# One more half of a depthwise convolution moved from TensorE to VectorE, one more sequence gated by sigmoid, and all instruction orders written anew

## The chip, the core and the metric

The kernel runs on one core of a Trainium2 chip. The core has five engines, each with its own in-order instruction queue: TensorE (PE) for matrix products and transposes, VectorE (DVE) and ScalarE (ACT) for elementwise work, GpSimd (POOL) for a few copies and for issuing loads, and SyncE (SP) for issuing DMAs. [...] The time is the device time of one execution in microseconds (us). Before the change it is 213.52 us, the median of three runs (213.04 to 213.94).

## The reference

Eight sequences (b = 0 to 7) of 576 rows go through attention with pooled keys and values, and then through a gated feed-forward block with a short convolution:

```python
k_p = k.reshape(B, H, Sp, 8, D).mean(axis=3)          # 576 keys -> 72
v_p = v.reshape(B, H, Sp, 8, D).mean(axis=3)
attn = softmax(scale * q @ k_p^T)                     # per head, 576 x 72
x = (attn @ v_p), the heads put side by side          # 576 x 512
h = np.maximum(x @ w_in, 0.0)                         # 576 x 1024
conv_out[s] = sum over k of conv_w[k] * h[s + k - 1]  # three taps, channel by channel
out = (h * 1 / (1 + exp(-conv_out))) @ w_out          # 576 x 512
```

Inputs and output are float32; the kernel computes in bfloat16 with float32 sums.

## The kernel before

**Tiles.** The sequences go in four pairs g = 0 to 3. Attention works on tiles (g, t) of 128 rows, nine or ten to a pair. One tile takes: scores on PE (line 607 when the array is used in quarters, line 620 when whole), the maximum on DVE (L633), the subtraction on DVE (L645) or, for pair 0, on PE (L653), exp on ACT (L682), a transpose by PE (L692) or by a DMA from SP (L701), the product with the pooled values on PE (L717), a reciprocal on DVE (L730), and the division on DVE (L745) or, as eight small instructions, on ACT (L738). The result x is transposed into xT.

**The feed-forward block.** The 1024 channels of a sequence are eight blocks fb of 128, in two halves f4 of four blocks. For each block PE computes the projection (`ffn_in`, L775, two times four matrix products), and ACT evicts it through a ReLU into hT (`ffn_relu`, L784). Then comes the convolution, in one of two ways:

- On PE (`ffn_conv`, L939): 32 small products by diagonal matrices for two blocks. ACT evicts them through tanh or sigmoid (L964), half of them into gT and half into a buffer tg, from which DVE brings them into gT (`ffn_gate`, L979 and L981).
- On DVE (`ffn_tap`, L911), for the halves listed in `Graph.TAPS`: two instructions for each block, h times a ratio of weights added to the running sum, which is held in float32 in tg. The rows of a sequence are interleaved, so the ends of hT must first get a copy of 63 columns from the other end (`ffn_wrap`, L859 and L860, one pair for two blocks, on POOL or ACT). ACT reads tg and writes the gate into gT (`ffn_tap_tanh`, L921).

The gate is a sigmoid. It is computed as tanh of half the argument, with the factor 0.5 put into the ReLU and a "+1" on DVE (L926 for tap halves, part of L979 and L981 otherwise), or, for the halves in `Graph.SIG`, as a sigmoid with no "+1". Exp and tanh are used under one activation table and sigmoid under another, so a sigmoid must stand behind every exp of the program; the last lines of the kernel add that dependence. `ffn_times` (L989) multiplies the gate by h, four blocks at once. When both halves of a sequence are gated, PE computes its output tiles (`ffn_out`, L997, eight products of 512 columns), DVE or ACT copies them out of PSUM (L1008), and SP or ACT issues the stores.

**Buffers and order.** Small rings of buffers are shared: three of tg, two of hT, two of gT. The program is a graph of operations. `Graph.ORDER` lists them in the order in which they are emitted, with the engine for each (a number is twice the operation's index plus the choice of engine, -1 is a filler product on PE, L424). `Graph.FORMS` sets the use of the PE array in whole or in parts, and `Graph.PLACES` the buffer of each operation. So the three tables fix each engine's queue. `pm`, `ident` and other constants are made in the first microseconds, while the first q and k arrive.

Of the kernel before, what the change touches and what calls it, by code (L numbers as in the profile page):

```python
# [33 lines left out]
class Graph:  # L34
# [25 lines left out]
    TAPS = ((4, 1), (5, 0), (5, 1), (6, 0), (6, 1), (7, 0), (7, 1))  # L60
# [8 lines left out]
    SIG = ((6, 0), (6, 1), (7, 0), (7, 1))  # L69
# [57 lines left out]
    )  # L127
    FORMS = (
        0, 0, 0, 0, 1, 1, 1, 1, 0, 0, 0, 0, 0, 1, 1, 0, 1, 1, 0, 0, 1, 0, 1, 0, 0, 0, 0, 1, 0, 0, 0, 1, 1, 1, 1, 1, 1, 1, 0, 1,
    )  # L130
    PLACES = (
# [51 lines left out]
def kernel(  # L183
# [1125 lines left out]
    def add_ffn(b, w):  # L1309
# [28 lines left out]
        for f4 in range(n_fb // 4 if b in Graph.WRAP else 0):  # L1338
            if (b, f4) not in Graph.TAPS and b not in Graph.SIXTEEN:
                continue  # L1340
# [7 lines left out]
        for f4 in range(n_fb // 4):  # L1348
            if (b, f4) not in Graph.TAPS:
                continue  # L1350
# [148 lines left out]
```

## Time and profile before

| | |
|---|---|
| median of 3 runs | 213.52 us (213.04 to 213.94) |
| the profiled execution | 213.68 us, its span 211.7 us |
| busy in the span | PE 198.9, DVE 190.5, ACT 167.2, POOL 36.7 us |
| granted TensorE clock, mean | 0.995 |
| HBM | 32.52 MB read, 9.44 MB written |

The span goes from the first instruction to the last. Busy time of an engine is the union of its instructions' durations; "xN" counts them, and a mean in ns is that of one instruction. In a row of a group, the part behind the second bar is the idle time of the engine just before these instructions and what ended it. A row of the windows view gives, for one stretch of time, its length and each engine's busy time in it, then the clock, the share of DMA time and the rate. A row of the chain or of the timeline gives start, length and what ran, with repeated instructions merged. "PEld" is the loading of weights, which overlaps PE's products.

### The profile page before, as it was taken

The numbers are of one execution on the slowest core, as the hardware profiler recorded it, in microseconds if no ns is written. First come the engines' busy times: TensorE is split into PE (matmuls) and PEld (weight loads), VectorE is DVE, ScalarE is ACT, GpSimd is POOL, SyncE is SP. The second block draws the span as 40 slices with busy tenths as digits, with TensorE's granted clock in tenths as the row PEclk, the third lists the DMA queues.
The fourth block names the chain that finished last, engine by engine and source line by source line (L and its number), as shares of the span: only waits on it lengthen the run. The fifth ranks groups of instructions, "written<-read, shape, count | busy, mean of one in ns | idle before, by whom it ended". The sixth has DMA issues, their size and how long they took to land.

```text
span 211.7 us, 6644 instructions
## 1 busy us (share of the span) xinstructions
PE 198.9 (94%) x2726; PEld 136.4 (64%) x2746; DVE 190.5 (90%) x338; ACT 167.2 (79%) x345; POOL 36.7 (17%) x60
## 2 busy tenths in 40 slices
PE   4899999999999999999999899999999999999990
PEld 1468788765688876776778675666666656654450
DVE  7879988999999999999998989999999999999520
ACT  2558677998999869999979977989899997889030
POOL 8604630052131110200000021000014400202000
PEclk9999999999999999999999999999999999999997
DMA  6999999999999999879663646756646626204985
GB/s 212 222 205 206 208 206 208 208 207 205 208 206 208 202 179 202 177 139 156 130 92 69 147 96 78 173 104 151 122 96 133 113 64 149 53 0 103 261 259 171
DMA packets 48834, 33.47 MB, mean 158 GB/s; under 512 B 28300, under 2 KB 43812, under 8 KB 48804
## 3 DMA queue, kind: packets, MB, share of 16 engines
q0 software_dynamic: 15216, 15.40, 44.6%
q1 hardware_dynamic: 32432, 15.93, 35.9%
q10 hardware_dynamic: 1156, 1.72, 2.8%
q8 instruction: 21, 0.34, 0.6%
q14 instruction: 9, 0.07, 0.1%
HBM read 32.52 MB, written 9.44 MB: 198 GB/s over the span
## 4 chain that ended last, share of the span: by engine, by line
PE 68%; DVE 19%; issue 5%; ACT 4%; DMA 2%; DVEq 0%; ACTq 0%
PE psum L997 25%; PE psum L775 22%; PE psum L717 5%; PE psum L939 3%; DVE negm L633 3%; DVE v L511 2%; PE psum L692 2%; DMA eT<-e 2%; PE psum L424 2%; DVE sd L645 2%; DVE gT L981 2%; PE psum L620 2%; DVE gT L989 1%; PE psum L653 1%; PE psum L762 1%
## 5 line engine op out<-in xcount | busy, mean ns | idle before, releaser
L775 PE MATMUL psum<-xT,w_in_sb 128*128 128x288 bf16 x512 | 72.0, 286 | 0.2
L997 PE MATMUL psum<-w_out_sb,gT 128*128 128x512 bf16 (+1 forms) x276 | 65.6, 373 | 1.4 <-issue 0.6
L775 PEld LDWEIGHTS <-w_in_sb 128*128 128x128 bf16 x512 | 47.8, 98 | 15.3
L784 ACT ACTIVATE hT<-psum 128x576 bf16<-128x576 f32 x64 | 41.1, 669 | 8.0 <-PE psum L775 7.8
L997 PEld LDWEIGHTS <-gT 128*128 128x128 bf16 x296 | 27.5, 98 | 26.5 <-DVE gT L989 0.5
L633 DVE TENSOR_REDUCE negm<-psum 128x8 f32<-128x576 f32 (+2 forms) x37 | 27.4, 750 | 2.0 <-ACT e L682 0.9
L921 ACT ACTIVATE gT<-tg,ratio 128x576 bf16<-128x576 f32 x28 | 21.6, 795 | 2.2 <-DVE tg L911 2.1
L911 DVE SCALAR_TENSOR_TENSOR tg<-hT,ratio,tg 128x576 f32<-128x576 bf16 x28 | 22.3, 813 | 0.7
L911 DVE SCALAR_TENSOR_TENSOR tg<-hT,ratio 128x576 f32<-128x576 bf16 x28 | 22.2, 812 | 0.2 <-ACT gT L921 0.2
L859 POOL COPY hT<-hT 128x126 bf16<-128x126 bf16 x7 | 5.7, 808 | 93.8 <-ACT hT L784 74.9
L989 DVE TENSOR_TENSOR gT<-gT,hT 128x2304 bf16<-128x2304 bf16 x16 | 21.6, 1354 | 0.2
L645 DVE TENSOR_TENSOR sd<-psum,negm 128x576 f32<-128x576 f32 x27 | 19.9, 751 | 0.6
L717 PE MATMUL psum<-vm,eT 128*128 128x65 bf16 (+5 forms) x240 | 19.0, 222 | 0.9 <-DMA eT<-e 0.9
L738 ACT ACTIVATE x<-psum,r 128x64 bf16<-128x64 f32 (+1 forms) x80 | 17.6, 352 | 2.8 <-DVE r L730 2.7
L682 ACT ACTIVATE e<-sd 128x576 bf16<-128x576 f32 x27 | 18.6, 703 | 0.4 <-DVE sd L645 0.2
L745 DVE TENSOR_TENSOR x<-psum,r 128x512 bf16<-128x512 f32 (+1 forms) x27 | 18.2, 682 | 0.5
L717 PEld LDWEIGHTS <-eT 128*128 128x128 bf16 (+1 forms) x240 | 15.1, 100 | 5.3 <-DMA eT<-e 1.7
L939 PE MATMUL psum<-hT,dw 64*64 64x288 bf16 (+2 forms) x576 | 17.0, 256 | 0.3 <-ACT qT L559 0.2
L939 PEld LDWEIGHTS <-dw 64*64 64x64 bf16 x576 | 13.9, 107 | 3.4 <-issue 2.3
L424 PE MATMUL psum<-gT 128*128 128x448 bf16 x40 | 13.1, 433 | 3.2 <-DVE gT L1106 2.8
L1008 ACT COPY osb<-psum 128x512 f32<-128x512 f32 x24 | 14.3, 600 | 1.2 <-PE psum L997 1.2
L511 DVE TENSOR_TENSOR v<-v 128x1280 bf16<-128x1280 bf16 (+2 forms) x24 | 12.9, 538 | 0.2
(95 smaller groups left out, 244.8 us busy)
## 6 DMA issues: line engine op xcount, KB each, us to landing
out_dram<-osb SPq DMA_DIRECT2D x54, 128.0 KB, 2.5
v<-in_v_dram POOLq DMA_DIRECT2D x8, 512.0 KB, 12.6
qp<-in_q_dram POOLq DMA_DIRECT2D x7, 576.0 KB, 15.3
kk<-in_k_dram POOLq DMA_DIRECT2D x3, 1152.0 KB, 13.7
out_dram<-qp ACTq DMA_DIRECT2D x12, 128.0 KB, 3.4
hT<-in_k_dram SPq DMA_DIRECT2D x2, 576.0 KB, 5.2
w_in_sb<-in_moe_w_in_dram POOLq DMA_DIRECT2D x2, 512.0 KB, 13.7
w_out_sb<-in_moe_w_out_dram POOLq DMA_DIRECT2D x1, 1024.0 KB, 23.7
```

The source lines that it names most:

```text
L633: nc.vector.tensor_reduce(out=a["m"][0:rows], in_=a["s"][0:rows, :, 0:2 * KW].rearrange("p a (h s) -> p a h s", s=Sp), axis=AX.X, op=OP.ma ...
L645: nc.vector.tensor_tensor(out=a["d"][0:rows], in0=a["s"][0:rows, :, 0:2 * KW].rearrange("p a (h s) -> p a h s", s=Sp), in1=a["m"][0:rows]. ...
L682: nc.scalar.activation(out=dst, in_=src, func=ACT.Exp,)
L717: nc.tensor.matmul(out=a["o"][lo:hi, h // 4, (h % 4) * (D + 1):(h % 4 + x1 - x0) * (D + 1)], lhsT=a["eT"][:, j, lo:hi], rhs=buf("vm", b)[: ...
L745: nc.vector.tensor_tensor(out=a["x"][0:rows].rearrange("p (a h d) -> p a h d", a=2, d=D), in0=ov[:, :, :, 0:D], in1=r[0:rows].unsqueeze(3) ...
L775: nc.tensor.matmul(out=banks(ps)[:, j, 0:SC], lhsT=w_in_block(dc, fb), rhs=buf("xT", g)[:, dc, i * S + j * SC:i * S + (j + 1) * SC], start ...
L784: nc.scalar.activation(out=h_of(b)[:, fb].rearrange("p (a s) -> p a s", a=2), in_=banks(ps)[:, :, 0:SC], func=ACT.Relu, scale=1.0 if (b, f ...
L911: nc.vector.scalar_tensor_tensor(out=acc, in0=h, scalar=w, in1=acc if tap else mid, op0=OP.mult, op1=OP.add)
L921: nc.scalar.activation(out=gate, in_=acc_of(b, fb, ps), func=squash(b, fb), scale=ratio[:, 1, fb:fb + 1])
L939: nc.tensor.matmul(out=banks(pss[r ^ c])[c * D:(c + 1) * D, j, lo:hi], lhsT=dw[r * D:(r + 1) * D, tap * n_fb + fb, :], rhs=hT[r * D:(r + 1 ...
L989: nc.vector.tensor_tensor(out=gate, in0=gate, in1=h_of(b)[:, four], op=OP.mult)
L997: nc.tensor.matmul(out=bank(ps)[0:rows, columns], lhsT=buf("gT", g)[:, fb, t * P:t * P + rows], rhs=w_out_sb[:, fb, columns], start=(fb == 0),
```

## The change

`Graph.TAPS` gets the half (4, 0): the first four blocks of sequence 4 are now convolved on DVE too, so that all eight halves of sequences 4 to 7 are. `Graph.SIG` gets both halves of sequence 5: their gates are sigmoids, so they stand behind every exp and need no "+1". `ORDER`, `FORMS` and `PLACES` are new from end to end. The tables are one line longer, so every line number behind them moves by one (L911 is L912 in the changed kernel).

```diff
-    TAPS = ((4, 1), (5, 0), (5, 1), (6, 0), (6, 1), (7, 0), (7, 1))
+    TAPS = ((4, 0), (4, 1), (5, 0), (5, 1), (6, 0), (6, 1), (7, 0), (7, 1))
...
-    SIG = ((6, 0), (6, 1), (7, 0), (7, 1))
+    SIG = ((5, 0), (5, 1), (6, 0), (6, 1), (7, 0), (7, 1))
...
     ORDER = (
-        0, 12, 10, 24, 16, 4, 44, 28, 8, 36, 14, 32, 46, 19, -1, -1, -1, -1, 21, 7,
...
+        0, 12, 10, 24, 16, 4, 44, 28, 8, 36, 14, 32, 46, 42, 40, -1, 66, -1, -1, -1,
...
```

Counted over the program, PE loses 64 convolution products, DVE gets 8 taps and loses one L926, one L979 and two L981; of the 16 pairs of wraps (14 before) POOL has 14 (7 before) and ACT 2 (7 before). PE has 40 fillers in both. The tables also deal out the copies and divisions that either DVE or ACT can do, as the prediction lists.

Two places in the queues. The first is ACT's queue where it changes from exp and tanh to sigmoid. gT_121 belongs to sequences 4 and 5 here, gT_122 to 6 and 7; e is the result of an exp, hT that of a ReLU, osb an output tile. Before:

```order
L738 ACTIVATE x_107<-psum,r_113 128x64 x8
L784 ACTIVATE hT_117<-psum 128x576
L1008 COPY osb_123<-psum 128x512
L921 ACT_TABLE_LOAD
L921 ACTIVATE gT_122<-tg_118,ratio 128x576
L784 ACTIVATE hT_117<-psum 128x576 x2
L859 COPY hT_117<-hT_117 128x2x63
L860 COPY hT_117<-hT_117 128x2x63
L1008 COPY osb_124<-psum 128x512
L921 ACTIVATE gT_122<-tg_119,ratio 128x576
```

After:

```order
L785 ACTIVATE hT_117<-psum 128x576 x3
L683 ACTIVATE e_98<-sd_130 128x2x2x144
L1009 COPY osb_126<-psum 128x512
L683 ACTIVATE e_101<-sd_129 128x2x2x144
L922 ACT_TABLE_LOAD
L922 ACTIVATE gT_121<-tg_118,ratio 128x576
L1009 COPY osb_125<-psum 128x512
L922 ACTIVATE gT_121<-tg_120,ratio 128x576
```

Before, the load of the table stands in the gates of pair 3 (gT_122), fifteen operations behind the last exp, and the copies at the ends of hT are among ACT's work. After, it stands directly behind the last exp, and the first sigmoids write gT_121: they are those of sequence 5.

The second place is DVE's queue where sequence 4 is gated. Before:

```order
L911 SCALAR_TENSOR_TENSOR tg_118<-hT_116,ratio 128x576
L730 RECIPROCAL r_111<-psum 128x8
L911 SCALAR_TENSOR_TENSOR tg_118<-hT_116,ratio,tg_118 128x576
L911 SCALAR_TENSOR_TENSOR tg_119<-hT_116,ratio,tg_119 128x576
L979 TENSOR_SCALAR gT_121<-gT_121 128x2x576
L981 TENSOR_SCALAR gT_121<-tg_120 64x2x576 x2
L989 TENSOR_TENSOR gT_121<-gT_121,hT_117 128x4x576
L633 TENSOR_REDUCE negm_96<-psum 128x8
```

After:

```order
L912 SCALAR_TENSOR_TENSOR tg_118<-hT_117,ratio 128x576
L912 SCALAR_TENSOR_TENSOR tg_120<-hT_116,ratio,tg_120 128x576
L646 TENSOR_TENSOR sd_130<-psum,negm_96 128x576
L912 SCALAR_TENSOR_TENSOR tg_119<-hT_117,ratio 128x576
L990 TENSOR_TENSOR gT_121<-gT_121,hT_116 128x4x576
L927 TENSOR_SCALAR gT_121<-gT_121 128x4x576
L912 SCALAR_TENSOR_TENSOR tg_120<-hT_117,ratio 128x576
L912 SCALAR_TENSOR_TENSOR tg_118<-hT_117,ratio,tg_118 128x576
L990 TENSOR_TENSOR gT_121<-gT_121,hT_116 128x4x576
L912 SCALAR_TENSOR_TENSOR tg_120<-hT_117,ratio,tg_120 128x576
```

Before, one half of sequence 4 arrives from PE's convolution and is brought into gT by an L979 and two L981, between taps of sequence 5 (hT_116) and ahead of maxima of attention. After (where hT_116 is sequence 4's and hT_117 sequence 5's), both halves have come by taps, a full-width "+1" (L927) and a product (L990) follow for each, and no attention stands between the two products.

More of the change, by code (lines that the diff above doesn't have):

```diff
@@ L72 @@
     ORDER = (
[54 rows of a table removed]
[55 rows of a table added]
     )
     FORMS = (
-        0, 0, 0, 0, 1, 1, 1, 1, 0, 0, 0, 0, 0, 1, 1, 0, 1, 1, 0, 0, 1, 0, 1, 0, 0, 0, 0, 1, 0, 0, 0, 1, 1, 1, 1, 1, 1, 1, 0, 1,
+        1, 1, 0, 0, 0, 0, 1, 0, 0, 0, 0, 1, 1, 1, 0, 0, 1, 0, 0, 0, 1, 1, 1, 0, 0, 0, 0, 1, 1, 0, 0, 1, 1, 1, 1, 1, 1, 1, 1, 0,
     )
     PLACES = (
[18 rows of a table removed]
[18 rows of a table added]
     )
```

143 rows, old and new, of tables (ORDER, PLACES) are left out of this document.

## The prediction

> **What bounds the kernel now.** I read the page's busy times first, then the chain, then the engines' busy time by stretch.
>
> ```profile
> span 211.7 us, 6644 instructions
> ...
> PE 198.9 (94%) x2726; PEld 136.4 (64%) x2746; DVE 190.5 (90%) x338; ACT 167.2 (79%) x345; POOL 36.7 (17%) x60
> ```
>
> ```profile
> PE 68%; DVE 19%; issue 5%; ACT 4%; DMA 2%; DVEq 0%; ACTq 0%
> ```
>
> Two engines are almost full, TensorE (PE, 94%) and VectorE (DVE, 90%), and ScalarE (ACT) isn't far behind. The chain is mostly PE's. A share of the span hides the stages, so here are the stretches that the chain's changes of engine suggest (time, its length, busy time of PE, its weight loads, DVE, ACT and POOL):
>
> ```profile
> 0.00:28.10 28.10, 24.41 (x434) 16.61 (x434) 23.68 (x64) 16.50 (x28) 14.56 (x27) 1.00 1.09 210
> 28.10:72.40 44.30, 43.58 (x734) 33.24 (x730) 42.33 (x82) 38.95 (x73) 9.02 (x17) 1.00 1.23 207
> 72.40:111.00 38.60, 37.72 (x677) 27.95 (x681) 37.74 (x65) 34.22 (x77) 2.47 (x3) 1.00 0.94 155
> ...
> 157.00:174.50 17.50, 17.39 (x119) 10.90 (x119) 17.29 (x26) 17.44 (x41) 4.75 (x6) 1.00 0.51 100
> ...
> 197.00:206.00 9.00, 8.82 (x48) 4.62 (x48) 3.08 (x6) 2.24 (x4) 0.00 (x0) 1.00 0.89 270
> 206.00:211.70 5.70, 0.00 (x0) 0.00 (x0) 0.34 (x1) 0.00 (x0) 0.00 (x0) 0.81 0.58 174
> ```
>
> The start (to 28.1) has room on every engine. From 28.1 to 72.4 PE is busy for 43.58 of 44.30; from 72.4 to 111.0 PE and DVE both miss less than a microsecond. After the last gate, at 197, PE works 8.8 us more on five tiles of output, and 5.7 us of copy and store end the span. Those two belong to the end whatever happens before it. The stretch that the change rebuilds runs from the first projection of sequence 4 (115.4) to the last gate (197):
>
> ```profile
> 0.00:115.40 115.40, 110.12 (x1948) 81.50 (x1957) 107.51 (x217) 93.72 (x183) 26.05 (x46) 1.00 1.06 184
> ...
> 115.40:197.00 81.60, 79.95 (x741) 50.27 (x742) 79.61 (x117) 71.29 (x159) 10.62 (x14) 1.00 0.54 108
> ```
>
> It lasts 81.60 us; PE works 79.95 of them and DVE 79.61. Neither leaves 2 us idle, ACT 10.3. So a microsecond taken from PE alone is worth nothing there unless DVE gets through as fast, and one put on DVE costs about one.
>
> **The change, part by part.** (1) TensorE loses the two convolution calls of sequence 4's first half. One call in the chain:
>
> ```profile
> 69.36 0.87 PE psum L939 x32
> ```
>
> The longest calls there take 0.94, this one 0.87; two are 1.7 us less on PE. In the rebuilt stretch PE then has 79.95 - 1.7 = 78.2 us of work. What hides the gain is DVE, next.
>
> (2) DVE gains eight tap instructions (line 911, two for each of four blocks), ACT gets four L921 activations out of SBUF in place of four out of PSUM, which is a few tenths. The half of sequence 4 loses its two-part gate (one L979, two L981) and takes a full L926; both L926 of sequence 5 go, since a sigmoid needs no "+1".
>
> ```profile
> L911 DVE SCALAR_TENSOR_TENSOR tg<-hT,ratio,tg 128x576 f32<-128x576 bf16 x28 | 22.3, 813 | 0.7
> L911 DVE SCALAR_TENSOR_TENSOR tg<-hT,ratio 128x576 f32<-128x576 bf16 x28 | 22.2, 812 | 0.2 <-ACT gT L921 0.2
> L921 ACT ACTIVATE gT<-tg,ratio 128x576 bf16<-128x576 f32 x28 | 21.6, 795 | 2.2 <-DVE tg L911 2.1
> ...
> L981 DVE TENSOR_SCALAR gT<-tg 64x1152 bf16<-64x1152 bf16 x18 | 8.9, 494 | 0.2
> ...
> L979 DVE TENSOR_SCALAR gT<-gT 128x1152 bf16<-128x1152 bf16 x9 | 4.0, 445 | 0.0
> ...
> L926 DVE TENSOR_SCALAR gT<-gT 128x2304 bf16<-128x2304 bf16 x3 | 2.3, 755 | 0.0
> ```
>
> The 56 taps overlap a little; by the windows view of that line they fill
>
> ```profile
> 0.00:211.70 211.70, 43.58 (x56) 0.99 0.84 158
> ```
>
> 43.58 / 56 = 0.78 us each. Eight: +6.2. Gates: -(0.45 + 2 x 0.49) - 0.76 = -2.2 (three L926 become two). Net +4.0 on DVE if nothing else moved.
>
> (3) The new order also deals out work between DVE and ACT anew. Inside the rebuilt stretch DVE drops three divisions (L745) and one output copy (L1008) to ACT, one maximum (L633) is done earlier, and one mask product (L515) falls into it:
>
> ```profile
> L633 DVE TENSOR_REDUCE negm<-psum 128x8 f32<-128x576 f32 x27 | 20.0, 750 | 0.7 <-ACT e L682 0.5
> ...
> L745 DVE TENSOR_TENSOR x<-psum,r 128x512 bf16<-128x512 f32 x26 | 17.6, 682 | 0.5
> L738 ACT ACTIVATE x<-psum,r 128x64 bf16<-128x64 f32 x72 | 15.9, 357 | 2.4 <-DVE r L730 2.3
> ...
> L515 DVE TENSOR_TENSOR vm<-v,mask_wide 128x960 bf16<-128x960 bf16 x8 | 5.2, 653 | 0.1
> ...
> L1008 DVE COPY osb<-psum 128x512 f32<-128x512 f32 x3 | 2.0, 682 | 1.2 <-DMA out_dram<-osb 1.2
> ```
>
> -3 x 0.68 - 0.68 - 0.75 + 0.65 = -2.8. Instructions overlap by some hundredths, so with (2) DVE has +1.2 to +1.5 in the stretch; I take +1.4. ACT gets three divisions of eight L738 each, which at 15.9 / 72 = 0.22 are +5.3, and loses five pairs of wraps, 0.6 each (part 5): about +2.4 on 71.3 of 81.6, still under PE and DVE over the whole stretch.
>
> So DVE has 79.61 + 1.4 = 81.0 us of work there and PE 78.2: DVE is the bound by itself. Its idle time decides the rest. At the old idle time, 81.60 - 79.61 = 2.0, the stretch takes 83.0 (+1.4); with none 81.0 (-0.6). Some of the old 2.0 came from waits for PE, which now has 2.8 us to spare, so I take 1.3 of idle and 82.3: +0.7. That is nearer to the upper end because an in-order queue of taps, ACT results and gates never ran without waits in any row above.
>
> (4) Before 115.4 the new order leaves the same attention and projections on PE, three score tiles in the quarter form instead of the full one and a key preparation in halves: a few tenths. DVE there takes two divisions and a maximum more (2 x 0.68 + 0.75), gives up two L770, one L706, one L515 and a pair of L559 (0.74 and a short one of about half its width, so about 0.4), and takes casts that ACT had: two L456 of full width, one L504, two L306 of qp, for one L306 of kk.
>
> ```profile
> L559 DVE COPY qT<-psum 128x1152 bf16<-128x1152 bf16 x4 | 3.0, 740 | 0.0
> L770 DVE COPY xT<-psum 128x512 bf16<-128x512 bf16 x7 | 2.9, 420 | 0.4 <-PE psum L762 0.2
> ...
> L706 DVE COPY eT<-psum 128x640 bf16<-128x640 bf16 x3 | 1.4, 483 | 0.0
> ...
> L504 ACT CAST kT<-psum 128x576 bf16<-128x576 f32 x2 | 1.3, 636 | 0.0
> ...
> L306 ACT CAST qp<-hT 128x512 bf16<-128x512 f32 x2 | 1.1, 615 | 3.7 <-DMA hT<-in_q_dram 3.7
> ...
> L306 DVE CAST kk<-hT 128x1152 bf16<-128x1152 f32 x1 | 1.0, 985 | 0.0
> ...
> L456 DVE CAST kT<-psum 64x144 bf16<-64x144 f32 x1 | 0.3, 299 | 0.9 <-PE psum L431 0.9
> ```
>
> The known ones are 2.1 - 0.84 - 0.48 - 0.65 - 1.15 = -1.0. Three forms have no row on DVE: L456 between 0.30 (half the width) and 0.6, L504 between ACT's 0.64 and 0.99, a qp cast between half of 0.99 and ACT's 0.62. That is 2 x 0.45 + 0.8 + 2 x 0.55 - 0.99 = +1.8 with the middles, +0.25 to +0.45 on either side. DVE: +0.8. It has 115.40 - 107.51 = 7.9 us idle there, most of it in the start, where those casts lie. Fully hidden it is 0, and the earlier first projection could give 0.5; not hidden it is +0.8. I take +0.2. POOL's loads come in another order (q of sequence 6 is last now), but all are issued before the rebuilt stretch. SP issues two more of the stores at the end and ACT two fewer; the DMA share of 0.54 in that stretch leaves room for either.
>
> (5) Wraps (lines 859 and 860). Before, 7 pairs ran on ACT and 7 on POOL; now 14 of 16 run on POOL, a queue with no other work by then.
>
> ```profile
> L859 ACT COPY hT<-hT 128x126 bf16<-128x126 bf16 x7 | 2.2, 310 | 0.1
> ```
>
> ```profile
> 156.34 0.29 POOL L860 COPY hT<-hT 128x126 bf16<-128x126 bf16 x1
> ...
> 190.02 0.88 POOL L859 COPY hT<-hT 128x126 bf16<-128x126 bf16 x1 [8.88 <-issue]
> ```
>
> A POOL copy takes 0.29 when it is alone and 0.88 beside taps, so a pair takes up to 1.8 us against 0.6 on ACT, and the tap behind it waits that much longer after its ReLU. In the order only two places have little between ReLU, wrap and tap (sequence 6's blocks 0 and 1, sequence 7's blocks 4 and 5): within the idle time of (3).
>
> Does POOL slow DVE? Two taps without a POOL copy beside them, two with, and the last gates:
>
> ```profile
> 188.35 1.54 DVE L911 SCALAR_TENSOR_TENSOR tg<-hT,ratio 128x576 f32<-128x576 bf16 x2
> 189.93 1.58 DVE L911 SCALAR_TENSOR_TENSOR tg<-hT,ratio,tg 128x576 f32<-128x576 bf16 x2
> ...
> 194.38 2.61 DVE L989 TENSOR_TENSOR gT<-gT,hT 128x2304 bf16<-128x2304 bf16 x2
> ```
>
> 1.54 against 1.58: 0.04 for two copies, so 14 more wrap copies cost DVE at most 0.3, in (3)'s idle time. [...]
>
> Sum: (3) +0.7, (4) +0.2, tail 0: +0.9 us on an execution of 213.68 (span 211.7 and 2.0 around it), 0.16 above the median of the runs. Against the median, 213.52 + 0.9 = **214.4 us**.
>
> **Rivals.** *DVE keeps pace (faster).* PE's lead lets DVE run nearly without waits: idle under 0.3 in the stretch (-0.3 to -0.6) and a start that is up to 0.5 to 1 us shorter, because the first projection stands a few operations earlier in the order. That gives 212.0 to 213.2. For it: PE gets 2.8 us of slack, and DVE managed 39.5 of 40.0 in the last stretch before 197. Against it: it needs DVE to be nearly perfect for 80 us. It decides when DVE's idle time there falls under 0.5.
>
> [...]
>
> *The sigmoid switch (slower).* All exps must precede the first sigmoid. Before, the switch came in sequence 6's gates, fifteen ACT operations after the last exp; now it stands right behind it, with
>
> ```profile
> L921 ACT ACT_TABLE_LOAD x1 | 1.3, 1283 | 0.0
> ```
>
> and sequence 5's gates behind that. The taps have three buffers, so DVE stops when three blocks wait for their activation. If the last two attention tiles come 1 to 3 us late, everything behind them does: 215 to 217. ACT was already busy for 17.44 of 17.50 from 157.0 to 174.5, where this lands.
>
> **How the numbers follow.** DVE-bound as summed, 213.4 to 215.6: 0.50. DVE keeps pace: 0.24. Wraps or ports: 0.13. Sigmoid switch: 0.08. Something in the start (load order, clock): 0.05. Half a per cent of the median, 1.07 us, is about what a measurement can tell, so faster means under 212.45 and slower over 214.59. The first case gives 0.28 the same and 0.22 slower; the second 0.20 faster and 0.04 same; the next two are slower (0.21); the last 0.02 faster, 0.03 slower. Faster 0.22, same 0.32, slower 0.46. The range 212.1 to 217.0 leaves a tenth outside at each end.
>
> **What would show it.** Right: L939 x512 and two calls fewer; 64 taps at 0.81; from sequence 4's first projection to the last gate 82 to 83 us with DVE over 98% busy and PE 2 to 4 us idle, its idle time released by DVE gT L990; a chain that runs through DVE to the last gate, then 8.8 + 5.7 us as before. Wrong: PE as full as before (the rival that keeps pace), DVE idle over 3 us with POOL hT or ACT gT as releaser (wraps, switch), or a first projection a microsecond away from 28.

## The result: 0.5% slower, with the loss and the gain in other places than predicted

The changed kernel takes 214.62 us (median of 20 runs, 213.20 to 216.68) beside 213.34 for the kernel before (20 runs, 212.73 to 214.66). The ratio is 1.0054 with an interval of 1.0028 to 1.0081. The profiled execution took 213.85 us, near the fast end of its runs, 0.17 more than the profiled one before. From its page, the span, the busy times and the chain by engine:

```profile
span 212.2 us, 6550 instructions
...
PE 198.1 (93%) x2668; PEld 135.1 (64%) x2688; DVE 191.5 (90%) x339; ACT 169.7 (80%) x345; POOL 44.1 (21%) x74
...
PE 59%; ACT 15%; DVE 11%; DMA 7%; issue 5%; SPq 1%; DVEq 0%; ACTq 0%
```

PE and DVE are about as full as before. The chain has more of ACT and of DMA in it and less of PE and of DVE (11% where it was 19%). The windows view by the prediction's stretches (time, length, busy time of PE, weight loads, DVE, ACT, POOL, then clock, DMA share and GB/s) shows where the time went:

```profile
0.00:117.99 117.99, 110.24 (x1966) 81.32 (x1975) 108.51 (x218) 93.41 (x168) 26.19 (x46) 1.00 1.06 183
117.99:198.00 80.01, 79.05 (x660) 49.19 (x666) 79.54 (x117) 74.49 (x174) 17.91 (x28) 1.00 0.53 112
198.00:207.00 9.00, 8.83 (x48) 4.62 (x48) 3.08 (x6) 1.76 (x3) 0.00 (x0) 1.00 0.87 229
207.00:212.20 5.20, 0.00 (x0) 0.00 (x0) 0.35 (x1) 0.00 (x0) 0.00 (x0) 0.97 0.52 152
```

| stretch of the profiled execution | before | after | predicted | measured |
|---|---|---|---|---|
| start to sequence 4's first projection | 115.40 | 117.99 | +0.2 | +2.6 |
| from there to the last gate (rebuilt) | 81.60 | 80.01 | +0.7 | -1.6 |
| tail | 14.7 | 14.2 | 0 | -0.5 |

These are one execution of each kernel, and two things have to be known to read them. In both, 20 of PE's products in `ffn_out` have no record (276 of 296), ten of them in the rebuilt stretch, so PE's busy time there reads about 0.6 us too low in both (the kernel with five entries changed, below, has them all and shows 79.64). And about half of the 1.6 us gained in the rebuilt stretch is a wait of the profiled execution before: PE waits 0.9 us there for a transposed eT by DMA, at 121 us. Two further kernels below, which are the kernel before with an edit, don't have that wait, and their stretch takes 80.73 and 80.75 us.

So in these two profiles the rebuilt stretch gained 1.6 us and the part ahead of it lost 2.6. In that first part PE has the same work as before (110.24 against 110.12) and 7.75 us of idle time in place of 5.28: 2.5 more. The waits of PE from sequence 0's first projection (27.75) on, after:

```profile
PE psum L608 <- issue: 1.5, 1, 1.5
PE psum L542 <- issue: 1.0, 1, 1.0
PE psum L763 <- ACT kT L484: 0.2, 1, 0.2
```

and before, over the same part of the work:

```profile
PE psum L997 <- issue: 0.5, 3, 0.2
PE psum L424 <- ACT kT L483: 0.3, 1, 0.3
```

Two single waits, 1.0 and 1.5 us, add up to the 2.5. "issue" means that nothing in the profile ended them. In the timeline of the longer one PE stops in the middle of one tile's scores, six products done and ten to go, and DVE then waits for PE:

```profile
91.20 0.25 PE L608 MATMUL psum<-kT,qT 64*64 64x72 bf16 x6
92.93 0.17 PEld L608 LDWEIGHTS <-qT 64*64 64x64 bf16 x10 [1.59 <-issue]
92.93 0.28 PE L608 MATMUL psum<-kT,qT 64*64 64x72 bf16 x10 [1.48 <-issue]
...
93.32 0.76 DVE L634 TENSOR_REDUCE negm<-psum 128x8 f32<-128x576 f32 x1 [1.41 <-PE psum L608]
```

**A cause that could be tried.** PE's own instructions may be what it waits for. The page lists a DMA queue of kind "instruction" (q8) with 21 packets of 0.34 MB in all, which is 16 KB each. PE's queue has 5377 instructions, which is 21 times 256 and one more, so one packet may be one page of 256. In the trace's DMA records one such packet is under way just ahead of each of the two stops; these are the rows of the DMA view from 43.90 to 44.95 and from 90.35 to 91.60:

```profile
q8 instruction: 1, 0.02, 5.8%
```

(the same row in both). The packets end at 44.90 and at 91.56, and PE goes on at 46.27 and at 92.93, which is 1.37 us later both times. The instructions that PE waits for are number 1471 and about number 3006 of its queue, six pages apart (1535 = 6 x 256 less one). That each packet brings PE one page is the author's reading of these counts and times, and the runs below test it.

At the pages that PE entered up to 121 us in this trace, the packet with the next page starts after the entry: at most 0.8 us after it from 99 to 121 us, and 1.2 to 3.8 us after it before that, where the loads and transposes keep the DMA engines full (a share of 1.29 from 86.56 to 90.39). The packet takes about 1 us (0.9 to 1.4 here), and 1.4 more pass at the two stops until PE goes on. So, as an estimate from these three times (3.8 + 1 + 1.4), a page has to last PE some 6 us while the DMA engines are full. The page that PE entered at 86.56 held one preparation of q in the quarter form and half of another, one score tile in that form and the first part of the next (a preparation has 72 instructions and a score tile 32, where the whole form has 36 and 8), a convolution call and projections. PE was through with it in 4.9 us. The kernel before has more instructions on PE, but the ends of its pages lie elsewhere. The closest page there was ready at 45.2 by the same count (its packet ended at 43.82, and 1.4 more), 0.3 us before PE came to it.

### The profile page after: what moved, and what is told of

Same layout as the page of the kernel before. It is cut to its first block, busy times and chain, and to the rows that moved or that the text cites. A ratio compares the mean times of both kernels' runs of the same rounds, so it can differ in the third digit from the quotient of the medians.

```text
span 212.2 us, 6550 instructions
## 1 busy us (share of the span) xinstructions
PE 198.1 (93%) x2668; PEld 135.1 (64%) x2688; DVE 191.5 (90%) x339; ACT 169.7 (80%) x345; POOL 44.1 (21%) x74
## 3 DMA queue, kind: packets, MB, share of 16 engines
q10 hardware_dynamic: 996, 1.45, 2.5%
## 4 chain that ended last, share of the span: by engine, by line
PE 59%; ACT 15%; DVE 11%; DMA 7%; issue 5%; SPq 1%; DVEq 0%; ACTq 0%
PE psum L998 19%; PE psum L776 19%; PE psum L940 4%; PE psum L718 4%; DMA hT<-in_k_dram 3%; DVE tg L912 3%; ACT gT L922 2%; PE psum L425 2%; DVE x L746 2%; PE psum L608 2%; ACT x L739 2%; PE psum L621 2%; ACT hT L785 2%; DMA eT<-e 2%; DMA out_dram<-osb 2%
## 5 line engine op out<-in xcount | busy, mean ns | idle before, releaser
L785 ACT ACTIVATE hT<-psum 128x576 bf16<-128x576 f32 x64 | 42.4, 690 | 6.9 <-PE psum L776 6.3
L860 POOL COPY hT<-hT 128x126 bf16<-128x126 bf16 x14 | 10.1, 719 | 91.0 <-ACT hT L785 79.9
L922 ACT ACTIVATE gT<-tg,ratio 128x576 bf16<-128x576 f32 x32 | 25.6, 825 | 2.2 <-DVE tg L912 2.2
L912 DVE SCALAR_TENSOR_TENSOR tg<-hT,ratio 128x576 f32<-128x576 bf16 x32 | 25.3, 815 | 0.1
L912 DVE SCALAR_TENSOR_TENSOR tg<-hT,ratio,tg 128x576 f32<-128x576 bf16 x32 | 25.1, 818 | 0.0
L990 DVE TENSOR_TENSOR gT<-gT,hT 128x2304 bf16<-128x2304 bf16 x16 | 21.5, 1348 | 0.3 <-ACT gT L922 0.2
L683 ACT ACTIVATE e<-sd 128x576 bf16<-128x576 f32 x27 | 19.7, 745 | 1.2 <-DVE sd L646 1.2
L739 ACT ACTIVATE x<-psum,r 128x64 bf16<-128x64 f32 (+1 forms) x88 | 19.6, 415 | 0.2 <-DVE r L731 0.2
L1009 ACT COPY osb<-psum 128x512 f32<-128x512 f32 x26 | 16.1, 623 | 4.5 <-PE psum L998 2.0
L940 PE MATMUL psum<-hT,dw 64*64 64x288 bf16 (+2 forms) x512 | 15.1, 256 | 0.2 <-ACT qT L560 0.2
L940 PEld LDWEIGHTS <-dw 64*64 64x64 bf16 x512 | 12.4, 107 | 2.0 <-issue 1.5
## 6 DMA issues: line engine op xcount, KB each, us to landing
kk<-in_k_dram POOLq DMA_DIRECT2D x3, 1152.0 KB, 14.7
```

What stands on the lines that cost most here:

```text
L739: nc.scalar.activation(out=a["x"][0:rows, n * D:(n + 1) * D], in_=ov[:, n // 4, n % 4, 0:D], func=ACT.Identity, scale=r[0:rows, n // 4, n ...
L785: nc.scalar.activation(out=h_of(b)[:, fb].rearrange("p (a s) -> p a s", a=2), in_=banks(ps)[:, :, 0:SC], func=ACT.Relu, scale=1.0 if (b, f ...
L912: nc.vector.scalar_tensor_tensor(out=acc, in0=h, scalar=w, in1=acc if tap else mid, op0=OP.mult, op1=OP.add)
L922: nc.scalar.activation(out=gate, in_=acc_of(b, fb, ps), func=squash(b, fb), scale=ratio[:, 1, fb:fb + 1])
L940: nc.tensor.matmul(out=banks(pss[r ^ c])[c * D:(c + 1) * D, j, lo:hi], lhsT=dw[r * D:(r + 1) * D, tap * n_fb + fb, :], rhs=hT[r * D:(r + 1 ...
L990: nc.vector.tensor_tensor(out=gate, in0=gate, in1=h_of(b)[:, four], op=OP.mult)
```

## The experiments

Two theories for the 2.6 us. **Instructions come late**: the two stops are ends of pages, and whatever moves the page ends or thins the work there moves the time. **The order itself**: DVE's extra work ahead of 118 and the new order of loads and stores cost the time, and page ends don't matter. Each ratio below is to the kernel before, run beside that kernel; the times themselves come from several sets of runs, so compare the ratios.

### Whole forms everywhere, in both kernels

The row of the changed kernel; the row of the kernel before gets the same zeros.

```diff
     FORMS = (
-        1, 1, 0, 0, 0, 0, 1, 0, 0, 0, 0, 1, 1, 1, 0, 0, 1, 0, 0, 0, 1, 1, 1, 0, 0, 0, 0, 1, 1, 0, 0, 1, 1, 1, 1, 1, 1, 1, 1, 0,
+        0, 0, 0, 0, 0, 0, 0, 0, 0, 0, 0, 0, 0, 0, 0, 0, 0, 0, 0, 0, 0, 0, 0, 0, 0, 0, 0, 0, 0, 0, 0, 0, 0, 0, 0, 0, 0, 0, 0, 0,
```

> The changed kernel with every entry of FORMS at 0: scores and preparations use the array whole or in halves, so TensorE has 4833 instructions in its queue instead of 5377; nothing else differs. Theory 'instructions come late': the changed kernel's trace has two places (45.27 to 46.27 and 91.45 to 92.93) where PE stops inside one operation for nothing that the profile shows, and both end 1.37 us after a 16 KB packet of the instruction queue; with fewer instructions to the microsecond both go away: 2.0 to 2.6 us less than the changed kernel in a profile, first projection of sequence 4 at 115.5 instead of 117.99, no stop of PE over 0.4 us without a releaser between 28 and 118. Rival 'the order itself' (DVE's extra work before 118 and the new order of loads and stores): the form of the products matters little, -0.3 to +0.5 us.

> The kernel before with every entry of FORMS at 0 (4961 instructions on PE instead of 5493). Theory 'instructions come late': by the page times of its trace no page of the kernel before came late (the closest arrived 0.3 us before it was needed, at 45), so there is nothing to gain: -0.3 to +0.5 us. A theory that the quarter forms are slow in themselves expects a gain here of the same size as in the changed kernel.

Measured: the changed kernel 215.26 us (1.0087, 1.0060 to 1.0114), the kernel before 215.64 (1.0108, 1.0082 to 1.0134). Both expectations on the time were wrong, because whole forms are dear in themselves (1.6 us of PE's time, below); that no stop would be left came out as expected. The windows from sequence 0's to sequence 4's first projection, the changed kernel and then the kernel before, with whole forms:

```profile
28.63:118.29 89.66, 88.68 (x1366) 66.94 (x1366) 85.13 (x155) 76.34 (x140) 14.84 (x24) 1.00 1.06 173
```

```profile
29.33:118.19 88.86, 87.84 (x1361) 66.43 (x1358) 84.15 (x153) 77.61 (x155) 10.69 (x18) 1.00 1.03 170
```

PE is busy for 88.68 us there in the changed kernel. With the given forms, the first kernel of the last part below, which is the same up to this point and whose profile has all of PE's products, shows

```profile
27.77:118.21 90.44, 87.05 (x1557) 65.34 (x1556) 85.13 (x155) 75.97 (x141) 14.83 (x24) 1.00 1.05 175
```

so the whole forms cost PE 1.6 us. With whole forms in both, the difference between the two kernels is -0.2% where it was +0.5%. PE's idle time in the two rows is 0.98 and 1.02 us, where it had been 2.2 us apart with the given forms, and the changed kernel's PE has no wait in the stretch that the view gives as more than 0.2 us. The stops are gone, and about 0.7% with them, some 1.6 us (the intervals of the ratios leave 0.4% on either side). The 0.8 us by which the changed kernel's stretch is still longer is busy time of PE: that much belongs to the order itself.

### The page ends moved

The fillers cut in two products of half the columns do the same work with more instructions, which moves every later page end. The first run cuts 18 of them, the second all 40 (40 in place of 18 in the edit).

```diff
     def fill(ps):
-        nc.tensor.matmul(out=bank(ps)[:, 0:448], lhsT=blank[:, 0:P], rhs=blank, start=True, stop=True)
+        fills.append(ps)
+        n = 2 if len(fills) <= 18 else 1
+        for i in range(n):
+            part = slice(i * 448 // n, (i + 1) * 448 // n)
+            nc.tensor.matmul(out=bank(ps)[:, part], lhsT=blank[:, 0:P], rhs=blank[:, part], start=True, stop=True)
```

> The changed kernel with the first 18 fillers cut into two products of 224 columns each: the same columns, 36 more instructions early in PE's queue, so every later page of 256 instructions ends 36 instructions earlier in the work. Theory 'instructions come late': carried forward through the page times of the trace, the stop at 45 grows to 1.6 us and the one at 91 to 3.3 (it then falls at about 90): 1.5 to 2.5 us slower than the changed kernel. Rival 'the order itself': no difference (within 0.3 us), the two stops stay as long as they were.

> The changed kernel with all 40 fillers cut into two: 80 more instructions than the changed kernel by the time of the second stop, and 44 more than with 18 cut. Theory 'instructions come late': the page ends move on to places with slower work, the stops shrink to about 0.7 and 0.2 us: 1.2 to 2.0 us faster than the changed kernel although more instructions are issued, and 3 to 4 us faster than with 18 cut. Rival 'the order itself': no difference. Rival 'each instruction costs': slower than with 18 cut, not faster.

With 18 cut the time is 213.18 us (0.9982, 0.9961 to 1.0003), with 40 cut 212.49 (0.9951, 0.9926 to 0.9976). The second came out close to what was expected against the changed kernel (2.1 us faster, forecast 1.2 to 2.0). The first did not: it was to be slower than the changed kernel and is faster by 1.4. PE stops in it at instructions 1471 and 2494 for 0.5 and 0.3 us, again at page ends (the sixth and the tenth), where 1.6 and 3.3 had been forecast at 45 and 90. A wait of 0.7 us at 89.2, also at a page end, is put down to a ReLU of ACT by the profile. The forecast had taken over the delay of each packet from the changed kernel. The packet for the page end at 89.8 now started 0.9 us after PE's entry, where it had been 3.8. So the page ends can be counted beforehand, but the packet's delay can't be carried from one kernel to the next.

With 40 cut the one stop without a releaser is 0.7 us long:

```profile
PE psum L946 <- issue: 0.7, 1, 0.7
```

It stands at instruction 3262, which is 7 x 256 less one behind number 1471. The gain over 18 cut is 0.7 us, where 3 to 4 had been forecast from the stops that didn't come. Not all of the gain over the changed kernel is the stops: in the profiles, 0.8 of 2.5 us lie ahead of sequence 0's first projection (26.98 against 27.75). Two further kernels check this from either side:

> The changed kernel once more, unchanged, to stand beside the other kernels of this set on the same chip. Both theories: 1.003 to 1.008 of the time before. Theory 'instructions come late': PE stops again at the same two instructions (the 1471st and about the 3006th of its queue, 6 and 12 pages of 256 less the same 65), for 0.5 to 1.5 us each.

> The kernel before with all 40 fillers cut into two products, the control for the run that cut those of the changed kernel. Theory 'instructions come late': no page of the kernel before is late with or without it, so within 0.5 us of the kernel before. Rival 'cutting the fillers helps the start of any kernel': 1 us or more faster, and then the gain of the changed kernel with cut fillers says nothing of pages.

The changed kernel again: 215.48 us (1.0111, 1.0082 to 1.0140), above the 1.003 to 1.008 expected, with the stops at the same two instructions:

```profile
PE psum L608 <- issue: 2.3, 1, 2.3
PE psum L542 <- issue: 1.0, 1, 1.0
```

The longer one took 1.5 us in the first profile and 2.3 in this one, since the packet began 4.6 us after PE's entry instead of 3.8. A stop that varies with its packet would fit runs spread from 213.2 to 216.7, though only two of these executions were profiled. The kernel before with its fillers cut is slower, 214.49 (1.0066, 1.0045 to 1.0087), where no difference had been expected. It has stops of 0.3, 0.4 and 0.2 us that it didn't have, at instructions 702, 1469 and 1724, the third, the sixth and the seventh page end. So cutting fillers doesn't help the start of any kernel by itself: here sequence 0's first projection comes at 28.62, later than the 28.10 before.

| kernel | instruction PE stops at, mod 256 | stop, us | packet ended | from there to PE's next product |
|---|---|---|---|---|
| changed | 1471, 191 | 45.27 to 46.27 | 44.90 | 1.37 |
| changed | 3006, 190 | 91.46 to 92.93 | 91.56 | 1.37 |
| changed, again | 1471, 191 | 45.31 to 46.31 | 44.98 | 1.33 |
| changed, again | 3006, 190 | 91.50 to 93.80 | 92.35 | 1.45 |
| changed, 18 cut | 1471, 191 | 44.15 to 44.68 | 43.19 | 1.49 |
| changed, 18 cut | 2494, 190 | 75.27 to 75.60 | 74.36 | 1.24 |
| changed, 40 cut | 3262, 190 | 93.20 to 93.86 | 92.23 | 1.63 |
| before, 40 cut | 702, 190 | 23.50 to 23.84 | 22.44 | 1.40 |
| before, 40 cut | 1469, 189 | 43.84 to 44.24 | 42.96 | 1.28 |
| before, 40 cut | 1724, 188 | 50.06 to 50.31 | 48.83 | 1.48 |

The numbers count along PE's queue (a record missing from a trace can shift one by two). Whatever stands there, convolution, scores or preparation, the place is the same: 65 to 68 short of a multiple of 256.

### The pages thinned just ahead of the stops

Four entries of FORMS, for two preparations of q and two score tiles between 85 and 91 us, and then a fifth, a preparation at 40 us:

```diff
     FORMS = (
-        1, 1, 0, 0, 0, 0, 1, 0, 0, 0, 0, 1, 1, 1, 0, 0, 1, 0, 0, 0, 1, 1, 1, 0, 0, 0, 0, 1, 1, 0, 0, 1, 1, 1, 1, 1, 1, 1, 1, 0,
+        1, 1, 0, 0, 0, 0, 1, 0, 0, 0, 0, 1, 1, 1, 0, 0, 1, 0, 0, 0, 1, 1, 1, 0, 0, 0, 0, 1, 1, 0, 0, 1, 0, 0, 0, 0, 1, 1, 1, 0,
...
     FORMS = (
-        1, 1, 0, 0, 0, 0, 1, 0, 0, 0, 0, 1, 1, 1, 0, 0, 1, 0, 0, 0, 1, 1, 1, 0, 0, 0, 0, 1, 1, 0, 0, 1, 1, 1, 1, 1, 1, 1, 1, 0,
+        1, 1, 0, 0, 0, 0, 1, 0, 0, 0, 0, 1, 1, 1, 0, 0, 0, 0, 0, 0, 1, 1, 1, 0, 0, 0, 0, 1, 1, 0, 0, 1, 0, 0, 0, 0, 1, 1, 1, 0,
```

> The changed kernel with four entries of FORMS at 0, those of two preparations of q and two score tiles between 85 and 95 us: 120 instructions fewer just ahead of the second stop, nothing changed before it. Theory 'instructions come late': the stop at 91.5 (1.48 us) goes, the one at 45 stays (about 1 us); the whole forms cost up to 0.4 us: 0.8 to 1.5 us faster than the changed kernel. Rival 'the order itself': 0 to 0.4 us slower.

> The changed kernel with five entries of FORMS at 0: the four of the run before (near 91 us) and one more, the preparation of q of sequence 3 at 40 us, 36 instructions fewer ahead of the first stop. Theory 'instructions come late': both stops of PE without a releaser (1.0 us at 45 and 1.5 at 91) are gone or under 0.3 us; 0.3 to 0.9 us faster than with four entries, so 211.5 to 212.2 where the kernel before has 213.4. Rival 'whole forms cost what they cost': 212.5 or more.

Four entries: 212.45 us (0.9960, 0.9937 to 0.9982), 0.9% or 2.0 us under the changed kernel by the ratios, more than the 0.8 to 1.5 us expected. Of PE's waits "L608 <- issue" is gone and the other stays:

```profile
PE psum L718 <- DMA eT<-e: 1.2, 1, 1.2
PE psum L542 <- issue: 0.8, 1, 0.8
```

The wait for eT, a transpose by DMA, is new in this profile, which is of the slowest of its 12 runs. Five entries: 212.02 us (0.9962, 0.9945 to 0.9979; 211.48 to 213.47), and neither stop is left. The time is in the forecast range, but against the kernel before beside it the fifth entry brought nothing that shows (0.9962 after 0.9960). PE's longest wait over the same part is

```profile
PE psum L425 <- ACT kT L484: 0.2, 1, 0.2
```

This is the changed kernel with five bits of a table turned. By the ratios it is 0.9% faster than the changed kernel was at first, some 2.0 us, and 1.5% faster than at its second measurement; and it is 0.4% faster than the kernel before. Its windows, to compare with the table at the top:

```profile
27.43:116.22 88.79, 87.71 (x1479) 66.39 (x1478) 85.15 (x155) 76.19 (x141) 14.86 (x24) 1.00 1.10 179
116.22:196.18 79.96, 79.64 (x670) 49.30 (x666) 79.53 (x117) 74.39 (x174) 17.61 (x28) 1.00 0.57 113
```

PE's idle time in the first is 1.08 us, beside 3.39 in the row of the given forms above, and its busy time 87.71 beside 87.05: the five whole forms cost 0.7. The stretch is 1.45 us shorter than in the profile at the top. The rebuilt stretch stays as it was.

The packet itself was no earlier. For the page that PE entered at 86.76 it started at 90.62, 3.9 us after the entry, as in the changed kernel (3.8). But with the whole forms the page lasted PE 7.2 us and not 4.9, and there was no stop. So between these two it is the time that the page lasts that made the difference.

> Both edits on the changed kernel: all fillers cut in two, and the four entries of FORMS at 0. Theory 'instructions come late': only about 0.7 us of a stop at 44 is left: 0 to 0.4 us faster than with the fillers cut alone, so 211.9 to 212.6 where the kernel before has 213.4. Rival 'the order itself': as the changed kernel or slower.

Cut fillers and four entries together gave 214.50 (1.0072, 1.0046 to 1.0098), where a gain had been expected. No page comes late in its profile. Instead PE waits in the rebuilt stretch for a transpose of x by DMA, at 136 us:

```profile
PEld L782 <- DMA xT<-x: 1.7, 1, 1.7
```

Why that transpose is late there stays open; its six runs lie between 214.01 and 215.43, but only one was profiled. Two edits that each take stops away needn't add up.

### What bounds the rebuilt stretch

The prediction had DVE as its only bound and PE with 2.8 us to spare. Three kernels price work on either, and on POOL. In the first, ORDER also gets the two "+1" operations (L927), each just ahead of its product on DVE.

```diff
-    SIG = ((5, 0), (5, 1), (6, 0), (6, 1), (7, 0), (7, 1))
+    SIG = ((6, 0), (6, 1), (7, 0), (7, 1))
```

> The changed kernel with the gates of sequence 5 by tanh again: two more '+1' instructions on DVE (0.67 each, 1.3 us) in the stretch from the first projection of sequence 4 to the last gate (80.0 us in the changed kernel), the table of the sigmoid loaded later. Theory 'DVE alone bounds the stretch' (the prediction's): 81.2 to 81.4. Theory 'PE and DVE bound it together': the same, since either is full. Theory 'PE bounds it': 80.0 to 80.3. Rival of the sigmoid switch (the early load of the table holds the gates of sequence 5 up): the stretch gets shorter, 79.0 to 79.8.

```diff
     def ffn_in(b, fb, j, ps):
-        for dc in range(n_dmc):
+        for dc in list(range(n_dmc)) * (2 if b == 5 and fb < 2 else 1):
```

> The changed kernel with the projection of two blocks of sequence 5 computed twice: 16 more products of 0.12 us, 1.95 us more on PE in the stretch of 80.0 us, and nothing more on DVE or ACT; about what the two convolution calls took (1.74). Theory 'DVE alone bounds the stretch': PE's slack takes most of it, 80.0 to 80.5. Theory 'PE and DVE bound it together': 81.2 to 82.0, and then the two calls that went were worth their time, which the prediction put at nothing.

```diff
     def ffn_wrap(b, lo, hi, copy):
         ...
+        if copy == nc.gpsimd.tensor_copy:
+            for _ in range(2):
+                copy(out=dw[:, 0:hi - lo, 0:TB - 1], in_=t[:, :, TB + 1:2 * TB])
```

> The changed kernel in which each pair of wraps on POOL is followed by two more copies of the same size, into a buffer that nobody reads any more: 28 more POOL copies beside the taps, and no tap waits for them. Theory 'a POOL copy does not hold DVE' (from 1.54 against 1.58 for two taps without and with two copies): taps at 0.81 to 0.83 us each, the stretch within 0.6 of 80.0. Rival 'a POOL copy holds DVE for its own 0.29 us': 28 times 0.29, so 8 us more in the stretch and a mean tap of 0.9 us.

The rebuilt stretch in the three, in this order:

```profile
118.21:199.51 81.30, 80.01 (x670) 49.28 (x666) 80.80 (x119) 74.86 (x174) 15.37 (x28) 1.00 0.53 111
```

```profile
117.59:199.20 81.61, 81.41 (x686) 50.85 (x682) 79.81 (x117) 74.60 (x174) 16.86 (x28) 1.00 0.55 110
```

```profile
117.96:198.43 80.47, 79.77 (x670) 49.31 (x666) 80.04 (x117) 74.54 (x174) 35.71 (x56) 1.00 0.53 113
```

1.3 us more on DVE cost 1.3 (81.30 against 80.01). The doubled projections put 1.8 us of busy time on PE (81.41 against the 79.64 of the five-entry kernel, both with all products on record) and cost 1.6 (81.61), and DVE's idle time went from 0.5 to 1.8 with it. As the theory that both engines bound the stretch had forecast, neither hides work put on the other: in the five-entry kernel PE is idle for 0.3 us of it and DVE for 0.4. Work taken from PE was not worth nothing. The kernel before shows the same from the other side. Its stretch in the profiles with whole forms and with cut fillers, neither of which has the wait for eT (the first has all of PE's products on record, the second lacks ten):

```profile
118.19:198.94 80.75, 80.60 (x738) 50.54 (x730) 79.35 (x117) 71.54 (x159) 10.65 (x14) 1.00 0.53 108
```

```profile
116.96:197.69 80.73, 79.95 (x740) 50.35 (x742) 79.32 (x117) 71.37 (x159) 10.62 (x14) 1.00 0.54 106
```

PE is busy for 80.60 of 80.75 us, and DVE is idle for 1.4. The cut fillers all lie ahead of this stretch, so nothing in it was edited in the second. By these rows PE alone bounded the stretch before the change. The change took 0.9 us from PE (79.95 to 79.05, both lacking ten products), and the stretch became 0.7 us shorter (80.73 to 80.01). The two stops at 45 and 91 are in all three profiles (0.9 to 1.0 and 1.5 to 1.7 us), so their whole times (214.94, 216.59 and 215.71 us, ratios 1.0062, 1.0175 and 1.0103) say less than the stretch. 28 more POOL copies cost 0.5 us, and the taps beside them are hardly longer than the changed kernel's 815 and 818 ns:

```profile
L915 DVE SCALAR_TENSOR_TENSOR tg<-hT,ratio 128x576 f32<-128x576 bf16 x32 | 25.6, 824 | 0.1
L915 DVE SCALAR_TENSOR_TENSOR tg<-hT,ratio,tg 128x576 f32<-128x576 bf16 x32 | 25.1, 819 | 0.0
```

## Why the prediction was right in its time and wrong in its reasons

The time, 214.4 us against a median of 214.62, came out close, with the ratio right at the border between no change and slower. That was luck: the rebuilt stretch was to lose 0.7 us and gained 1.6 in the profiles, the part ahead of it was to lose 0.2 and lost 2.6, and the two errors nearly cancelled.

- **(1) PE's 1.7 us, "DVE is the bound by itself": wrong.** The reading that PE left 1.65 us idle there before the change was the first mistake: 0.9 of it was one wait of that execution, and some 0.6 the ten products without a record. PE had no room. The wait, here as PE's weight loads have it, is for a transposed eT:

```profile
PEld L717 <- DMA eT<-e: 1.2, 1, 1.2
```

  PE's busy time in the stretch fell by 0.9, not by 1.7 (why it wasn't more stays open), and that shortened the stretch, by 0.7 when it is set against the profile of the kernel before that lacks the wait. A microsecond put on PE costs 0.9 there (1.6 of 1.8), by the run that computes two projections twice, so what comes off it isn't hidden by DVE.
- **(2) Eight taps, +6.2: mis-sized.** The taps' busy time by the windows view of their line:

```profile
0.00:212.20 212.20, 48.85 (x64) 1.00 0.84 158
```

  48.85 - 43.58 = 5.3 for eight, 0.66 each and not 0.78. Taps that stand back to back overlap more: at the end of the stretch they start 0.73 us apart (eight from 189.55 to 195.39). The mean of the old ones, many of which stood between other instructions, was too dear.
- **(3) DVE in the stretch, +1.4 of work and 1.3 of idle time left: wrong in both.** The moved divisions, the copy, the maximum and the mask came as counted. DVE's work didn't grow at all (79.61 to 79.54); 0.9 of the 1.4 is the taps, and the rest wasn't followed up. Its idle time fell from 2.0 to 0.5, just where the rival "DVE keeps pace" had put its point of decision. The stretch was to take 82.3 and took 80.0. The reason given for leaving idle time, that no row showed such a queue without waits, was wrong: DVE's one wait of note in the stretch is 0.2 us for a gate.
- **(4) The part before, +0.2: the step that failed.** DVE's work grew by 1.0 there (0.8 predicted). The quarter forms were written down as "a few tenths" of PE's time. What they do to the number of instructions in a page wasn't asked, and two page ends stopped PE for 2.5 us in the profile.
- **(5) Wraps on POOL: right.** The 14 pairs leave the taps at 815 and 818 ns (812 and 813 before), and 28 more copies beside them cost 0.5 us. Had each held DVE for its own 0.29 us, that would have been 28 x 0.29 = 8.1. What is slower here is POOL's copy, 719 ns in the mean of one line against 0.29 us alone: 17 of the 56 copies of that run take 0.79 to 0.83 us, as long as one tap (0.82). So POOL's copies got longer beside the taps and the taps hardly did; why was not tried. What the prediction's chances call "Wraps or ports" (0.13), wraps that come late or POOL copies that hold DVE, didn't come: the one wait of DVE that the view gives in the changed kernel's stretch is 0.2 us, for ACT.
- **The sigmoid switch: rightly held small.** Taking sequence 5's sigmoids back costs the "+1" instructions (the stretch takes 81.30 us in place of 80.01) and gains nothing.
- **The start: right.** The first projection stands at 27.75, and the prediction had allowed a microsecond either side of 28.
- **The tail** is 0.5 us shorter, in the copy and store at its end (5.2 against 5.7), which the prediction left unchanged.

Of the rivals, "DVE keeps pace" has DVE's idle time in the rebuilt stretch right, but not its reason: PE had no lead, it stayed as full as DVE, as the prediction's own sign of being wrong says. Its time did not come because of a cost in another part that no rival had. "Two pages late" should have been the rival on the slow side.

## To carry to other kernels

A new order or another form of the same products changes which instructions fall into one page, so count PE's instructions against time where the DMA engines are full: here a page of 256 that PE was through with in 4.9 us, beside a DMA share of 1.29, made PE wait, and one that lasted 7.2 us didn't. Every stop here of over 0.2 us in the middle of PE's work with "issue" as its releaser was such a page end, always at the same place modulo 256 (188 to 191), and a few products in the whole form just ahead of the two in the changed kernel took them away. Look, too, at how many of an engine's records a profile has, and at whether its largest wait comes again in another profile, before its idle time is counted as room. In a stretch where two engines are both over 97% busy, a microsecond on either cost most of itself (1.3 us for 1.3 on DVE, 1.6 for 1.8 on PE), so neither may be put down at nothing.

## Not expected of the hardware

PE resumed 1.24 to 1.63 us after the packet with its instructions had ended, in all 17 stops of over 0.2 us at page ends, in nine executions (the ten in the table, and seven at the same two instructions in the kernel with four entries and in the last three). In the two profiles of the changed kernel, at the pages entered up to 121 us, a packet started from 0.1 us after PE's entry into a page (at 100 us) to 4.6 us after it (at 87 us, with a DMA share of over 1). That the load on the DMA engines is what delays it fits most packets, but not each (0.5 us beside a share of 1.2 in the kernel before, at 91 us), and no run changed that load alone. The stop's length varies from one execution to the next of the same kernel (1.5 and 2.3 us, in executions of 213.85 and 215.09 us).
